# Attention and mixture of experts on one core: five pieces of zeros leave the loop, the table of slots goes through PSUM, one weight pass changes engine

## The chip, the core and the metric

The kernel runs on one NeuronCore of a Trainium2 chip. The core has TensorE (PE), which multiplies matrices into PSUM; VectorE (DVE), ScalarE (ACT) and GpSimd (POOL), which work element by element; and SyncE (SP), which here only issues DMAs. PEld is the load of PE's weights. Each engine takes its instructions in their written order and waits at semaphores; a q behind a name (SPq, POOLq) is the engine's sequencer. The metric is device time in microseconds (us), the median of the timed runs.

## The reference

Two stages. The first is attention with decay, one state per head of 64 x 64:

```
state = gamma * state + k[t] v[t]^T          # gamma per head, for each t of 768
y[t]  = scale * q[t] state                   # 4 batches, 8 heads, head size 64
```

The heads are put side by side to x, 3072 rows of 512. The second stage sends every row to two of eight experts:

```
logits = x @ w_gate;  noisy = logits + log1p(exp(x @ w_noise)) * noise
top2   = the two largest of noisy;  g = softmax over these two
out[row] = sum over the two of  g * ( relu(x[row] @ w1[e]) @ w2[e] )     # 512 -> 1024 -> 512
```

## The kernel before

**The loop.** Attention runs in 24 iterations (`for j in range(NCH)`), one for 128 time steps; six of them make a batch. An iteration issues, in this order: `qk(j+1)`, the product of k and scaled q for the next chunk (PE, L365); `q_scale(j+2)` (qs, POOL, L346) and `v_scale(j+1)` (vp, POOL, L340); the loads of chunk j+4 (SP, L278); `masked(j+1)` (am, DVE, L372); `x_store(j-3)` (SP, L428); `y_in(j)` (PE, L378); `x_total(j-1)` and `x_hi(j-1)`, the scale and the upper half of x (ACT, L412); then what the table `between` holds for this iteration; `y_mm(j)`, which adds the state's part and updates the state (PE L386 and L396, ACT L391 and L402); `x_rows(j-2)`, the transposes of x (PE L422, ACT L424) and `logits(j-2)` (PE L435 and L438); `slip()`, which issues a waiting `x_lo` (DVE, L416); then the tables `todo` and `late`. The lists are filled before the loop, so the order on every engine is written out by hand.

**What rides along.** Routing of a finished batch is cut into steps `route_a` to `route_f` and laid into later iterations, by the number `n` of the batch's last one. `table(b)` multiplies one-hot tables on PE into `LST` in PSUM (L584); `route_f(b)` adds that to `acc`, the table of slots (56 columns, SBUF); `rows_of` turns columns of it into `idx`, the row numbers that the gathers use (L599 to L602). The first weights are scaled and split as well: `w_hi` (ACT), then for each quarter of w1 `w_scaled` on POOL (L228), in place, and `w_rest` on POOL (L232).

**Zeros.** The outputs are added to by scattering DMAs, so they must hold zeros first. `zero_out(i)` writes one of twelve pieces of 512 KB from a tile of zeros, on SP's queue (L307). Eight are issued in iterations 7 and 11 to 17, four in the stage behind the loop.

**Behind the loop** the first expert's blocks follow as `units` (`early(n)` issues n of them): `mm1` on columns 0 to 384 (eight units), `mm2` for three blocks, `mm1` on columns 384 to 576 (eight), `mm2` again. Between these the last batch is routed, the other blocks are gathered (xg, POOL) and transposed by DMA into xe (SP, L709), and the next weights are loaded. Then come the seven other experts, `mm1s` and `mm2`.

**Tiles of PSUM.** `pL` is one bank that holds the logits (`PL`), the positions, `LST`, and the sums `SUM` and `XSS`; `pR` is another, in which DVE keeps small tables; its rows on the trace carry these names. On SP each DMA waits for the DMA that was issued eight before it (its lane, DMAHW0 to 7).

Of the kernel before, what the change touches and what calls it, by code (L numbers as in the profile page):

```python
# [10 lines left out]
F32 = mybir.dt.float32  # L11
# [5 lines left out]
OP = mybir.AluOpType  # L17
# [21 lines left out]
NBLK, CAP = 7, 832  # L39
CAPS = [832, 832, 832, 832, 800, 800, 768, 768]  # L40
NCOL = NBLK * E
# [54 lines left out]
def moe_kernel(ctx, tc, qT, kT, kt, vt, noise, wgn, w1, w2, ctab, qtab, xbuf, gbuf, out):  # L96
    nc = tc.nc
# [5 lines left out]
    work = ctx.enter_context(tc.tile_pool(name="work", bufs=2))  # L103
# [15 lines left out]
    def K(n):  # L119
        return ct[:, _C[n][0]:_C[n][1]]  # L120
# [10 lines left out]
    acc = consts.tile([128, NCOL], F32, name="acc")  # L131
# [12 lines left out]
    pR = psum.tile([128, 512], F32, name="pR")  # L144
# [3 lines left out]
    LST = pL[:, 280:280 + NCOL]  # L148
# [9 lines left out]
    wide = pR[:, 144:144 + NC * NL].rearrange("p (c e) -> p c e", c=NC)  # L158
    small = pR[:, 208:208 + 48]
    second_best = pR[:, 256:256 + NC]  # L160

    def pow2(ss, target, up, down=None):

# [263 lines left out]
    def x_store(j):  # L427
        nc.sync.dma_start(xbuf[128 + j * C:128 + (j + 1) * C, :], XR.pop(j))  # L428
# [158 lines left out]
    def route_f(b):  # L587
        if b == 0:
            nc.vector.tensor_copy(acc, LST)
        else:  # L590
            nc.vector.tensor_tensor(acc, acc, LST, op=OP.add)

    tk = consts.tile([128, NCOL], F32, name="tk")

    def rows_of(tk, n0, n1):

        padv = work.tile([128, NCOL], F32, name="padv")
        neg = work.tile([128, NCOL], F32, name="neg")
        nc.vector.tensor_scalar(padv[:, n0:n1], tk[:, n0:n1], 0.0, K("pad"), op0=OP.is_equal, op1=OP.mult)  # L599
        nc.vector.tensor_scalar(neg[:, n0:n1], tk[:, n0:n1], 0.0, float(TOK), op0=OP.is_lt, op1=OP.mult)  # L600
        nc.vector.tensor_tensor(neg[:, n0:n1], neg[:, n0:n1], padv[:, n0:n1], op=OP.add)
        nc.vector.scalar_tensor_tensor(idx[:, n0:n1], tk[:, n0:n1], 127.0, neg[:, n0:n1], op0=OP.add, op1=OP.add)  # L602

    def ranks():

        nc.vector.tensor_copy(cum, cump)
        m = E - 2
        n, s3, s4 = R["cum"][:, 2:E], [128, m, m], [128, m, NBLK, m]
        key = hp.tile([128, m], F32, name="key")
        nc.vector.scalar_tensor_tensor(key, n, 8.0, K("tie")[:, :m], op0=OP.mult, op1=OP.add)  # L610
        cm = hp.tile(s3, F32, name="cm")
        nc.vector.tensor_tensor(cm, key[:, None, :].to_broadcast(s3), key[:, :, None].to_broadcast(s3), op=OP.is_gt)
        rk = hp.tile([128, m], F32, name="rk")
        nc.vector.tensor_reduce(rk, cm, axis=AX.X, op=OP.add)
        pm = R["pm"] = hp.tile(s3, F32, name="pm")
        nc.vector.tensor_tensor(pm, rk[:, None, :].to_broadcast(s3),
                                K("i64")[:, :m, None].to_broadcast(s3), op=OP.is_equal)
        nc.vector.tensor_tensor(cm, pm, K("lidx")[:, None, 2:E].to_broadcast(s3), op=OP.mult)
        nc.vector.tensor_reduce(rk, cm, axis=AX.X, op=OP.add)
        nc.vector.tensor_copy(eid[:, :m], rk)  # L620
        tp = hp.tile(s4, F32, name="tp")
        v = acc[:, 2 * NBLK:].rearrange("p (e t) -> p t e", e=m)
        nc.vector.tensor_tensor(tp, v[:, None].to_broadcast(s4), pm[:, :, None, :].to_broadcast(s4), op=OP.mult)
        nc.vector.tensor_reduce(tk[:, 2 * NBLK:].rearrange("p (r t) -> p r t", r=m), tp, axis=AX.X, op=OP.add)
        rows_of(tk, 2 * NBLK, NCOL)
        nc.vector.tensor_tensor(cm, pm, K("rcap")[:, 1:, None].to_broadcast(s3), op=OP.mult)
        nc.vector.memset(capd, float(CAP))
        nc.vector.tensor_reduce(capd[:, 2:E], cm.rearrange("p r e -> p e r"), axis=AX.X, op=OP.add)
# [40 lines left out]
    def at(j, f, *a):  # L669
        todo.setdefault(j, []).append((f, a))  # L670
# [42 lines left out]
    for b in range(B - 1):  # L713
        n = (b + 1) * NC - 1
        late.setdefault(n + 2, []).append((route_a, (b,)))
        late.setdefault(n + 4, []).append((route_n, (b,)))
        steps = [(3, route_b, b), (4, route_b2, b), (4, route_c, b), (5, route_d, b),
                 (6, route_e, b, 0), (7, route_e, b, 1), (8, route_w, b)]
        if b == B - 2:
            steps = steps[:-2]  # L720
        else:
            at(n + 8, table, b)
            late.setdefault(n + 8, []).append((route_f, (b,)))
        if b == B0 - 1:

            late[n + 8].append((rows_of, (acc, 0, 3)))
            for t in range(3):
                ahead_of.setdefault(n + 9, []).append((gather, 0, t, 0, 128, B0 * S))
                at(n + 10, x_t, 0, t)
        ahead_of.setdefault(n + 5, []).append((places, b))  # L730
        for s in steps:
            between.setdefault(n + s[0], []).append(s[1:])
# [5 lines left out]
    for i in range(4):  # L738
        at(3 + i, w_load, 0, "1", i)
        at(5 + i, w_sum, 0, "1", i)  # L740
        at(10 + i, w_hi, 0, "1", i)
        between.setdefault((11, 13, 16, 18)[i], []).append((w_scaled, nc.gpsimd, 0, "1", i))
        between.setdefault((12, 14, 17, 19)[i], []).append((w_rest, 0, "1", i))
        at(8 + i, w_load, 0, "2", i)
        at(14 + i, w_sum, 0, "2", i)
        at(19 + i, w_hi, 0, "2", i)
    at(23, w_scaled, nc.scalar, 0, "2", 0)
    at(22, w_load, 1, "1", 0, 2)
    at(22, w_load, 1, "1", 2, 2)
    for i in range(8):  # L750
        at((7, 11, 12, 13, 14, 15, 16, 17)[i], zero_out, i)
    for i in range(2):
        at(10, zero_out, 12 + i)
    for j, a in ((4, (lanes16, K("lanes"))), (4, (blks16, K("blks"))), (5, (lanes.bitcast(F32), lanes16.bitcast(F32))),
# [13 lines left out]
    for j in range(NCH):  # L768
        if j == 0:
            y_in(0)  # L770
        if j + 1 < NCH:
            qk(j + 1)
        if j + 2 < NCH:
            q_scale(j + 2)
        if j + 1 < NCH:
            v_scale(j + 1)
        if j + AHEAD < NCH:
            load(j + AHEAD, "qk")
        if j + 1 < NCH:
            masked(j + 1)  # L780
        if j + AHEAD < NCH:
            load(j + AHEAD, ("v", "kt"))
        if j >= 3:
            x_store(j - 3)
        if j:
            y_in(j)
            for f, *a in ahead_of.get(j, []):
                f(*a)
            x_total(j - 1)
            x_hi(j - 1)  # L790
            slips.append(j - 1)
        for f, *a in between.get(j, []):
            f(*a)
        if j < NC - 3:
            q_table(j + 3)
        y_mm(j)
        if j >= 2:
            x_rows(j - 2)
            logits(j - 2)
        slip()  # L800
        for f, a in todo.get(j, []):
            f(*a)
        for f, a in late.get(j, []):
            f(*a)
# [251 lines left out]
    x_rows(NCH - 1)  # L1056
    logits(NCH - 1)
    x_store(NCH - 1)
    table(b - 1)
    route_f(b - 1)  # L1060
    rows_of(acc, 3, mid + 1)
    for t in range(3, mid + 1):
        gather(0, t, 0, min(128, SECOND - t * 128), (B - 1) * S)
    for t in range(3, mid + 1):
# [32 lines left out]
    early(1)  # L1097
    table(b)
    route_f(b)
    rows_of(acc, mid, 2 * NBLK)  # L1100
    for t in range(mid, NBLK):
        gather(0, t, SECOND - t * 128 if t == mid else 0)
    for t in range(mid, NBLK):
# [248 lines left out]
```

## Time and profile before

| | |
|---|---|
| three timed runs | 637.21, 634.17, 636.15 us; median 636.15 |
| profiled execution | 632.04 us, of which the trace's span is 630.3 |
| busy of the span | PE 97%, PEld 61%, DVE 72%, ACT 62%, POOL 63% |
| bytes moved | 112.90 MB, mean 179 GB/s |
| TensorE clock | 0.996 of full speed on average |
| the loop | from 0 to about 115 us |

A busy PE is not PE at its peak: its matmuls are pipelined and their ends are modelled. What a stage is worth is read from the waits in it and from how long equal pieces of work take, not from the share. A wait is put down to the last semaphore by the trace, which may hide a DMA behind an engine's name.

### The profile page before, as it was taken

How to read it: one execution, taken by the hardware profiler on the slowest of the kernel's cores; microseconds unless marked ns; L12 is line 12 of the kernel's file. 1: busy time of each engine (PE TensorE's matmuls, PEld its weight loads, DVE VectorE, ACT ScalarE, POOL GpSimd, SP SyncE). 2: the span in 40 equal slices, each digit the busy share in tenths (PEclk: the TensorE clock that was granted, in tenths of full speed). 3: DMA queues.
4: the chain of work that ended last, by engine and by line, in shares of the span. 5: the costliest groups of instructions: out<-in, count | busy, mean ns of one | idle time of the engine just before them, and what ended most of it. 6: DMA issues, size and time to landing. Idle time of an engine off the chain costs nothing.

```text
span 630.3 us, 13242 instructions
## 1 busy us (share of the span) xinstructions
PE 611.6 (97%) x5133; PEld 384.9 (61%) x5133; DVE 451.2 (72%) x952; ACT 391.8 (62%) x655; POOL 395.2 (63%) x278
## 2 busy tenths in 40 slices
PE   8999988999999999999999999999999999999995
PEld 5899877756755545554565446544654565445784
DVE  5679888788697795579657964796579557957720
ACT  4788877944456856586558655865586558556311
POOL 2657889525776885863687558657845674574154
PEclk9999999999999999999999999999999999999998
DMA  9999999867972597479546974787499549642043
GB/s 332 350 404 405 355 384 317 244 222 208 195 193 36 85 258 226 55 133 243 161 49 118 197 229 56 169 201 176 46 146 216 160 54 162 192 52 35 9 52 44
DMA packets 104321, 112.90 MB, mean 179 GB/s; under 512 B 64512, under 2 KB 78080, under 8 KB 100672
## 3 DMA queue, kind: packets, MB, share of 16 engines
q1 hardware_dynamic: 83296, 84.70, 45.5%
q0 software_dynamic: 20528, 26.90, 27.3%
q8 instruction: 41, 0.67, 0.4%
q10 hardware_dynamic: 432, 0.43, 0.2%
q14 instruction: 24, 0.20, 0.1%
HBM read 72.16 MB, written 26.47 MB: 156 GB/s over the span
## 4 chain that ended last, share of the span: by engine, by line
PE 83%; DVE 8%; DMA 3%; ACT 2%; issue 1%; POOL 1%; SPq 1%; POOLq 0%; ACTq 0%; DVEq 0%
PE pO L1001 11%; PE pO L1002 11%; PE pO L1003 11%; PE pH L900 11%; PE pH L902 10%; PE pH L901 10%; PE pA L365 2%; DVE am L372 2%; PE pY L378 2%; PE pO L992 2%; PE pT L1016 2%; PE pO L990 1%; PE pO L991 1%; PE pH L824 1%; DMA in_q<-qT 1%; PE pH L826 1%
## 5 line engine op out<-in xcount | busy, mean ns | idle before, releaser
L977 POOL DMA_INDIRECT out<-ot,idx x108 | 196.1, 1816 | 139.3 <-ACT ot L971 47.8
L1002 PE MATMUL pO<-w2l,h 128*128 128x512 f16 x336 | 127.3, 379 | 0.0
L1003 PE MATMUL pO<-w2h,h 128*128 128x512 f16 x336 | 127.3, 379 | 0.0
L1001 PE MATMUL pO<-w2h,h 128*128 128x512 f16 x336 | 127.3, 379 | 0.0
L924 DVE TENSOR_TENSOR s<-pH,s 128x416 f32<-128x416 f32 (+2 forms) x84 | 47.3, 571 | 45.0 <-PE pH L902 36.7
L697 POOL DMA_INDIRECT gx<-gbuf,idx x54 | 60.9, 1128 | 28.1 <-issue 14.5
L687 POOL DMA_INDIRECT xg<-xbuf,idx x55 | 59.2, 1076 | 20.6 <-issue 15.1
L971 ACT ACTIVATE ot<-pO,gse 128x512 f32<-128x512 f32 (+2 forms) x48 | 32.7, 683 | 59.5 <-PE pO L1003 55.9
L191 ACT ACTIVATE junk<-wst 128x1024 bf16<-128x1024 f32 x64 | 67.8, 1060 | 2.9 <-DMA wst<-w 2.8
L920 ACT ACTIVATE s<-pH 128x416 f32<-128x416 f32 (+2 forms) x84 | 40.2, 508 | 30.7 <-PE pH L902 30.6
L916 ACT ACTIVATE h<-s 128x832 f16<-128x832 f32 (+2 forms) x42 | 35.9, 871 | 35.1 <-DVE s L924 35.1
L1003 PEld LDWEIGHTS <-h 128*128 128x128 f16 x336 | 32.9, 98 | 39.7
L1001 PEld LDWEIGHTS <-h 128*128 128x128 f16 x336 | 33.0, 98 | 38.8
L1002 PEld LDWEIGHTS <-h 128*128 128x128 f16 x336 | 32.9, 98 | 38.8
L902 PE MATMUL pH<-xt,wsl 128*128 128x416 f16 (+2 forms) x168 | 56.0, 333 | 0.0
L901 PE MATMUL pH<-xt,wsh 128*128 128x416 f16 (+2 forms) x168 | 56.0, 333 | 0.0
L900 PE MATMUL pH<-xt,wsh 128*128 128x416 f16 (+2 forms) x168 | 56.0, 333 | 0.0
L220 DVE SCALAR_TENSOR_TENSOR w2l<-wst,wsc,w2h 128x1024 f16<-128x1024 f32 x28 | 35.9, 1281 | 14.1 <-ACT w2h L215 14.1
L346 POOL TENSOR_TENSOR qs<-in_q,gq 128x512 f32<-128x512 f32 x21 | 26.7, 1273 | 26.3 <-DMA in_q<-qT 17.2
L917 DVE SCALAR_TENSOR_TENSOR h<-s,h 128x832 f16<-128x832 f32 (+2 forms) x42 | 41.0, 990 | 2.7 <-ACT h L916 2.7
L858 ACT ACTIVATE xt<-s 128x832 f16<-128x832 f32 (+2 forms) x28 | 24.4, 874 | 25.1 <-DVE s L857 24.9
L900 PE MATMUL pH<-xe,w1h 128*128 128x416 f16 (+2 forms) x112 | 37.3, 333 | 0.1
(217 smaller groups left out, 1477.7 us busy)
## 6 DMA issues: line engine op xcount, KB each, us to landing
wst<-w SPq DMA_DIRECT2D x28, 1024.0 KB, 7.9
in_q<-qT SPq DMA_DIRECT2D x24, 256.0 KB, 5.7
in_k<-kT SPq DMA_DIRECT2D x24, 256.0 KB, 6.4
in_v<-vt SPq DMA_DIRECT2D x24, 256.0 KB, 5.7
xbuf<-xr SPq DMA_DIRECT2D x24, 256.0 KB, 5.6
out<-zero SPq DMA_DIRECT2D x12, 512.0 KB
in_kt<-kt SPq DMA_DIRECT2D x20, 256.0 KB, 4.5
wst<-w SPq DMA_DIRECT2D x8, 512.0 KB, 6.4
```

Of the source, the lines that this page charges most:

```text
L191: nc.scalar.activation(junk, st[:, i * 1024:(i + 1) * 1024], AF.Square, accum_out=ss[:, i:i + 1])
L687: nc.gpsimd.indirect_dma_start(out=x[:p1], out_offset=None, in_=xbuf[:128 + rows], in_offset=bass.IndirectOffsetOnAxis(ap=idx[:p1, i:i + 1 ...
L697: nc.gpsimd.indirect_dma_start(out=GX[e][:, t, :], out_offset=None, in_=gbuf[:128 + rows], in_offset=bass.IndirectOffsetOnAxis(ap=idx[:, i ...
L900: nc.tensor.matmul(p, wh, bh[:, k, :], start=start and k == 0, stop=False, skip_group_check=True)
L901: nc.tensor.matmul(p, wh, bl[:, k, :], start=False, stop=False, skip_group_check=True)
L902: nc.tensor.matmul(p, wl, bh[:, k, :], start=False, stop=(k == 1), skip_group_check=True)
L917: wait.append(lambda: nc.vector.scalar_tensor_tensor(lo, src, 0.0, hi, op0=OP.max, op1=OP.subtract))
L924: nc.vector.tensor_tensor(s[:, u], p, s[:, u], op=OP.add)
L977: nc.gpsimd.indirect_dma_start(out=out[s], out_offset=bass.IndirectOffsetOnAxis(ap=idx[:n, i:i + 1], axis=0), in_=ot[:n, s * HD:(s + 1) * ...
L1001: nc.tensor.matmul(p, a, WT["2h"][:, f, :], start=(f == 0), stop=False)
L1002: nc.tensor.matmul(p, a, WT["2l"][:, f, :], start=False, stop=False)
L1003: nc.tensor.matmul(p, c, WT["2h"][:, f, :], start=False, stop=(f == FT - 1))
```

## The change

Of the eight pieces of zeros in the loop three stay (iterations 7, 13 and 16), and five are issued behind the loop, right after the last `x_store`. `route_f` writes the sum of `acc` and `LST` to `accp`, 56 columns of `pR` in PSUM, for every batch but the first; `rows_of` and `ranks` read it there, and the inner product `padv` of `rows_of` becomes `padp`, in PSUM too. After the second and third batch `accp` is copied back to `acc`. The last of the four `w_scaled` of w1 is issued on ACT, in the same iteration. Last, `logits(0)` is issued in iteration 3, ahead of `logits(1)`, where it was issued in iteration 2.

```diff
@@ PSUM views @@
+    accp = pR[:, 264:264 + NCOL]
+    padp = pR[:, 264 + NCOL:264 + 2 * NCOL]
@@ route_f @@
-            nc.vector.tensor_tensor(acc, acc, LST, op=OP.add)
+            nc.vector.tensor_tensor(accp, acc, LST, op=OP.add)
@@ rows_of @@
-        padv = work.tile([128, NCOL], F32, name="padv")
-        nc.vector.tensor_scalar(padv[:, n0:n1], tk[:, n0:n1], 0.0, K("pad"), op0=OP.is_equal, op1=OP.mult)
+        nc.vector.tensor_scalar(padp[:, n0:n1], tk[:, n0:n1], 0.0, K("pad"), op0=OP.is_equal, op1=OP.mult)
         nc.vector.tensor_scalar(neg[:, n0:n1], tk[:, n0:n1], 0.0, float(TOK), op0=OP.is_lt, op1=OP.mult)
-        nc.vector.tensor_tensor(neg[:, n0:n1], neg[:, n0:n1], padv[:, n0:n1], op=OP.add)
+        nc.vector.tensor_tensor(neg[:, n0:n1], neg[:, n0:n1], padp[:, n0:n1], op=OP.add)
@@ ranks @@
-        v = acc[:, 2 * NBLK:].rearrange("p (e t) -> p t e", e=m)
+        v = accp[:, 2 * NBLK:].rearrange("p (e t) -> p t e", e=m)
@@ tables of the loop @@
-            late[n + 8].append((rows_of, (acc, 0, 3)))
+            late[n + 8].append((rows_of, (accp, 0, 3)))
+            between.setdefault(n + 9, []).append((nc.vector.tensor_copy, acc, accp))
-        between.setdefault((11, 13, 16, 18)[i], []).append((w_scaled, nc.gpsimd, 0, "1", i))
+        between.setdefault((11, 13, 16, 18)[i], []).append((w_scaled, nc.scalar if i == 3 else nc.gpsimd, 0, "1", i))
-    for i in range(8):
-        at((7, 11, 12, 13, 14, 15, 16, 17)[i], zero_out, i)
+    for i in range(3):
+        at((7, 13, 16)[i], zero_out, i)
@@ the loop @@
-            logits(j - 2)
+            for i in (() if j == 2 else (0, 1) if j == 3 else (j - 2,)):
+                logits(i)
@@ behind the loop @@
     x_store(NCH - 1)
+    for i in range(3, 8):
+        zero_out(i)
     table(b - 1)
     route_f(b - 1)
-    rows_of(acc, 3, mid + 1)
+    rows_of(accp, 3, mid + 1)
+    nc.vector.tensor_copy(acc, accp)
...
-    rows_of(acc, mid, 2 * NBLK)
+    rows_of(accp, mid, 2 * NBLK)
```

On DVE, iteration 19 and the start of iteration 20, where the second batch's table becomes row numbers (names ahead of the arrow are written, those behind it read). Before:

```order
L591 TENSOR_TENSOR acc<-acc,pL 128x56 [waits PE_49]
L599 TENSOR_SCALAR padv<-acc,ct 128x3 [waits DVE_49]
L600 TENSOR_SCALAR neg<-acc 128x3
L601 TENSOR_TENSOR neg<-neg,padv 128x3 [waits DVE_49]
L602 SCALAR_TENSOR_TENSOR idx<-acc,neg 128x3 [waits DVE_49]
L454 TENSOR_SCALAR pR<-upx 128x6
L457 COPY lg<-pL 128x96
L458 TENSOR_TENSOR lg<-lg,pL 128x96 [waits DVE_49]
```

And now:

```order
L593 TENSOR_TENSOR pR<-acc,pL 128x56 [waits PE_49]
L600 TENSOR_SCALAR pR<-pR,ct 128x3 [waits DVE_49]
L601 TENSOR_SCALAR neg<-pR 128x3 [waits DVE_49]
L602 TENSOR_TENSOR neg<-neg,pR 128x3 [waits DVE_49]
L603 SCALAR_TENSOR_TENSOR idx<-pR,neg 128x3 [waits DVE_49]
L456 TENSOR_SCALAR pR<-upx 128x6 [waits DVE_49]
L459 COPY lg<-pL 128x96
L460 TENSOR_TENSOR lg<-lg,pL 128x96 [waits DVE_49]
```

The steps keep their places; no step of `rows_of` has both its source table and its target in SBUF any more, and two steps have a wait for DVE itself that they had not. The copy back stands some steps later, ahead of the next batch's noise product.

On POOL, iterations 17 to 20, from the third `w_rest` of w1 to the first gather. Before:

```order
L232 TENSOR_TENSOR w1l<-wst_496,w1h 128x2x512 [waits Pool_49]
L346 TENSOR_TENSOR qs<-in_q,gq 128x512 [waits DMAHW2_49,PE_49]
L340 TENSOR_TENSOR vp<-in_v,ct 128x512 [waits DMAHW6_49]
L228 TENSOR_SCALAR wst_496<-wst_496,wsc_498 128x1024 [waits Activation_49]
L346 TENSOR_TENSOR qs<-in_q,gq 128x512 [waits DMAHW0_49,PE_49]
L340 TENSOR_TENSOR vp<-in_v,ct 128x512 [waits DMAHW4_49]
L232 TENSOR_TENSOR w1l<-wst_496,w1h 128x2x512 [waits Pool_49]
L346 TENSOR_TENSOR qs<-in_q,gq 128x512 [waits DMAHW6_49,PE_49]
L340 TENSOR_TENSOR vp<-in_v,ct 128x512 [waits DMAHW2_49]
L687 DMA xg<-xbuf,idx 128x1024 [waits DMAHW3_49,DMAHW7_49,DMAHW1_49,DVE_49]
```

And now:

```order
L234 TENSOR_TENSOR w1l<-wst_496,w1h 128x2x512 [waits Pool_49]
L348 TENSOR_TENSOR qs<-in_q,gq 128x512 [waits DMAHW6_49,PE_49]
L342 TENSOR_TENSOR vp<-in_v,ct 128x512 [waits DMAHW3_49]
L348 TENSOR_TENSOR qs<-in_q,gq 128x512 [waits DMAHW4_49,PE_49]
L342 TENSOR_TENSOR vp<-in_v,ct 128x512 [waits DMAHW0_49]
L234 TENSOR_TENSOR w1l<-wst_496,w1h 128x2x512 [waits Activation_49]
L348 TENSOR_TENSOR qs<-in_q,gq 128x512 [waits DMAHW1_49,PE_49,Pool_49]
L342 TENSOR_TENSOR vp<-in_v,ct 128x512 [waits DMAHW6_49,Pool_49]
L688 DMA xg<-xbuf,idx 128x1024 [waits DMAHW7_49,DMAHW5_49,DVE_49]
```

The pass over wst is gone from POOL, and the last `w_rest` waits for ACT where it waited for POOL.

On SP, behind the loop, from the last stored rows (`xbuf<-xr`) to the loads of the next expert's w2. Before:

```order
L428 DMA xbuf<-xr 128x1024 [waits DMAHW3_49,Activation_49]
L709 DMA_TRANSPOSE xe<-xg 128x8x128 [waits DMAHW4_49,DMASW6_49]
L709 DMA_TRANSPOSE xe<-xg 128x8x64 [waits DMAHW5_49,DMASW7_49]
L187 DMA wst_2523<-w 128x2048 [waits DMAHW6_49,Pool_49]
L187 DMA wst_2523<-w 128x2048 [waits DMAHW7_49]
```

And now:

```order
L430 DMA xbuf<-xr 128x1024 [waits DMAHW6_49,Activation_49]
L309 DMA out<-zero 256x1x512 [waits DMAHW7_49]
L309 DMA out<-zero 256x1x512 [waits DMAHW0_49]
L309 DMA out<-zero 256x1x512 [waits DMAHW1_49]
L309 DMA out<-zero 256x1x512 [waits DMAHW2_49]
L309 DMA out<-zero 256x1x512 [waits DMAHW3_49]
L710 DMA_TRANSPOSE xe<-xg 128x8x128 [waits DMAHW4_49,DMASW6_49]
L710 DMA_TRANSPOSE xe<-xg 128x8x64 [waits DMAHW5_49,DMASW7_49]
L189 DMA wst_2523<-w 128x2048 [waits DMAHW6_49,Pool_49]
L189 DMA wst_2523<-w 128x2048 [waits DMAHW7_49]
```

The five pieces stand between the last stored rows and the transposes of blocks 3 and 4.

## Rows read from the trace of the kernel before

**Rows 1.** The page's 40 slices of the span: busy tenths of TensorE, of the DMA engines.

```profile
PE   8999988999999999999999999999999999999995
DMA  9999999867972597479546974787499549642043
```

**Rows 2.** Windows: from:to, length, busy us (instructions) of five engines, clock, DMA share, GB/s.

```profile
33.41:58.21 24.80, 24.80 (x471) 23.22 (x470) 20.21 (x84) 22.45 (x47) 13.18 (x13) 1.00 1.04 405
58.21:85.37 27.16, 25.16 (x481) 23.30 (x480) 23.02 (x95) 22.73 (x45) 22.73 (x15) 1.00 1.06 370
85.37:114.25 28.88, 24.54 (x467) 22.51 (x466) 26.63 (x107) 22.31 (x45) 25.96 (x21) 1.00 1.04 326
160.00:620.00 460.00, 459.88 (x2903) 260.88 (x2902) 325.25 (x490) 277.50 (x424) 294.63 (x199) 1.00 0.67 133
```

**Rows 3.** Timeline of TensorE, the table: start, duration, instruction, count, [idle before, releaser].

```profile
95.88 0.47 PE L584 MATMUL pL<-bb,a 128*128 128x56 f16 x12
```

**Rows 4.** Chain of waits, 73 to 84 us: start, duration, what.

```profile
73.74 7.12 DMA in_q<-qT
...
82.32 1.16 PE pA L365 x16
```

**Rows 5.** Waits of TensorE, 58 to 116 us: total us, times, longest.

```profile
PE pA L365 <- POOL qs L346: 3.9, 6, 1.2
PE pL L407 <- DVE lg L458: 1.9, 1, 1.9
PE pH L824 <- DMA xe<-xg: 0.7, 1, 0.7
PE pY L378 <- DVE x L416: 0.4, 1, 0.4
```

**Rows 6.** Timeline of GpSimd, iterations 18 and 19.

```profile
92.62 2.85 POOL L228 TENSOR_SCALAR wst<-wst,wsc 128x1024 f32<-128x1024 f32 x1
95.43 1.28 POOL L346 TENSOR_TENSOR qs<-in_q,gq 128x512 f32<-128x512 f32 x1
...
97.66 2.14 POOL L232 TENSOR_TENSOR w1l<-wst,w1h 128x1024 f16<-128x1024 f32 x1
```

**Rows 7.** Timeline of VectorE, `rows_of` twice, and a step from PSUM to PSUM.

```profile
97.22 2.60 DVE L599 TENSOR_SCALAR padv<-acc,ct 128x3 f32<-128x3 f32 x1
99.74 0.15 DVE L600 TENSOR_SCALAR neg<-acc 128x3 f32<-128x3 f32 x1
...
112.04 0.16 DVE L550 TENSOR_SCALAR pR<-pR 128x1 f32<-128x1 f32 x1
...
125.42 1.12 DVE L599 TENSOR_SCALAR padv<-acc,ct 128x2 f32<-128x2 f32 x1
```

**Rows 8.** Timeline of ScalarE: copy of iteration 18, and a `w_scaled` of w2.

```profile
92.80 1.02 ACT L424 ACTIVATE xr<-pX 128x1024 f16<-128x1024 f16 x1 [0.73 <-DMA xbuf<-xr]
...
116.78 1.16 ACT L226 ACTIVATE wst<-wst,wsc 128x1024 f32<-128x1024 f32 x1
```

**Rows 9.** Chain of waits, from the first gather to the first `mm1`.

```profile
102.59 4.90 DMA xg<-xbuf,idx
...
110.85 4.75 DMA xe<-xg
115.74 0.32 PE pH L824
```

**Rows 10.** Timeline of TensorE, iterations 2 and 3.

```profile
20.58 0.19 PE L435 MATMUL pL<-wg,x 128*128 128x32 f16 x1 [0.57 <-DVE p2m L167]
...
20.87 1.16 PE L365 MATMUL pA<-qs,in_k 64*128 64x128 f32 x16
...
22.36 1.09 PE L378 MATMUL pY<-am,vp 128*64 128x128 f32 x16 [0.33 <-DVE x L416]
```

**Rows 11.** Timeline of SyncE and TensorE: transposes of blocks 3 and 4, their first use.

```profile
130.59 2.55 SPq L709 DMA_TRANSPOSE xe<-xg  x2
...
150.76 0.25 PE L824 MATMUL pH<-xe,w1h 128*128 128x192 f16 x1
```

## The prediction

> **What bounds the kernel now.** I read the 40 slices first [rows 1]. TensorE (PE) stands at 8 or 9 everywhere, so busy shares say little by themselves; the DMA row is at 9 over the first seven slices, which is the attention loop of 24 iterations, and moves about below that afterwards. Then I cut the loop into equal pieces: the windows of [rows 2] begin with the transposes of iterations 5, 11, 17 and 23, so each of the first three holds six iterations, one batch each. They last 24.80, 27.16 and 28.88 us. In the first PE is busy to the last hundredth, and its 24.80 us are what six iterations need; the last row shows 459.88 of 460 us busy between 160 and 620. So PE sets the pace up to 58 us and again behind the loop, and between the two it waits. A microsecond that the loop loses there is a microsecond of the end, and one that is won is won at the end, as long as the stage behind it keeps its place.
>
> What the second and third batch need of PE: the first one's 24.80, and 0.47 for one table product that the first has not [rows 3], 25.3; the third has one qk product less (1.16 [rows 4]), 24.1. They lose 27.16 - 25.3 = 1.9 and 28.88 - 24.1 = 4.8 us. Who is waited for stands in [rows 5]: POOL's qs six times (3.9 us), the lg of VectorE (DVE) once (1.9), the loop's transposed rows xe at the loop's end (0.7), x_lo (0.4): 6.9 us, which agrees with 1.9 + 4.8.
>
> Behind POOL's qs stands another cause each time. At 73.74 the chain of waits goes through the load of a q, 7.12 us to its landing, then POOL's qs, and into qk at 82.32 [rows 4]: that is the DMA queue, at a share of 1.04 to 1.06 in all three batches [rows 2]. Later it is POOL itself: w_scaled of 2.85 us, then qs at once behind it at 95.43 [rows 6], POOL being busy 25.96 of 28.88 us. And lg was late because DVE stood in padv for 2.60 us [rows 7].
>
> **The change part by part.** *Five pieces of zeros leave the loop.* Each is 0.52 MB, at the 405 GB/s of the first batch 1.3 us of the DMA engines. By the iterations that issued them four lie in the second batch and one in the third. The second moved 370 GB/s x 27.16 us = 10.0 MB; without four pieces 7.9 MB, or 19.6 us at 405 GB/s, and this is below the 25.3 us of PE. The third: 326 x 28.88 = 9.4 MB, less 0.5, 22 us. So the loads no longer bind in either. What is late next in the second batch: DVE and POOL have 23.0 and 22.7 us of work in it [rows 2], both under PE's need, so PE is next, with the one x_lo wait of 0.4 us left. I take 25.3 + 0.4 = 25.7 us, a gain of 1.4; ends: 0 (the waits only change their owner) and 1.9.
>
> *w_scaled of piece 3 goes from POOL to ScalarE (ACT).* POOL loses 2.85 us in iteration 18 [rows 6], and qs of iteration 19 can start as soon as its q has landed. On ACT the same form took 1.16 us [rows 8]. ACT is busy 22.31 of 28.88 us in that batch, and it waited 0.73 us for a store just after, in iteration 18 [rows 8], so it has room; but the copies queued behind it (the square sum, U, xr) come 1.1 us later. U is used by the next iteration's y_mm, which stands behind its qk and y_in; I cost this at nothing, and at up to 1.1 us if that cover is gone.
>
> *The table through PSUM.* padv is DVE's tensor_scalar on three columns, SBUF to SBUF, and took 2.60 us at 97.22 and 1.12 us at 125.42, where the next one of the same form, neg, took 0.15 [rows 7]. It began while POOL worked without a pause and ended at 99.82, when POOL's w1l ended (97.66 + 2.14 = 99.80) [rows 6]; it is a wait for POOL, not work. With source and target in PSUM, the nearest row is 0.16 us for a tensor_scalar from pR to pR [rows 7]. So 2.44 us go in iteration 19. Added are one copy of 56 columns (0.16, by the same row) and two more waits of DVE for itself, about 0.1 each, an estimate from neg, which has no such wait and began 0.08 before padv's end (99.74 against 99.82). Net -2.1 us of DVE. Bounds: if PSUM helped nothing, 0 and +0.4; if all waiting goes, -2.4. The second place, 1.12 us, is hidden: its gather has 14 us in hand (below), so nothing there.
>
> [...]
>
> The third batch then. DVE is its fullest engine: 26.63 of 28.88 us, 24.5 after the change, more than the 24.1 of PE. It also stood 2.25 us idle for partners (ACT's x_hi, PE's qk); most of that is order of work and stays, I take 1.8. So 24.5 + 1.8 = 26.3, rounded to 26.4: a gain of 2.5, ends 0.5 (only a part of the padv stall, the rest taken by the later w_scaled) and 4.8 (PE's need).
>
> *End of the loop.* The first gather goes out at 102.59 behind POOL's work of iteration 20, lands after 4.90 us, three transposes follow, and mm1 starts at 115.74 [rows 9], of which PE idled 0.7 [rows 5]. Its index comes 2.4 us earlier and POOL is 2.85 us lighter, so this chain shortens its start by more than the loop shortens its end: I take 0.6 of the 0.7; ends 0 and 0.7.
>
> *The logits of row block 0 move from iteration 2 to 3.* In iteration 2 they waited 0.57 us for DVE and took 0.29 (20.58 to 20.87); but y_in at 22.36 waited for x_lo, not for them [rows 10]. So they cost nothing there, and in iteration 3, where PE is the bound, they cost 0.29. I take +0.3; ends 0 and 0.3.
>
> *The five pieces behind the last stored rows.* 2.6 MB, 6.5 us. They are issued on SP's queue at about 126, ahead of the transposes of blocks 3 and 4 (issued 130.59 to 133.14). The DMA row stands at 6 in that slice [rows 1]. mm1 reads these blocks first at 150.76 [rows 11]. With the 4.75 us that a transpose took under load [rows 9] they were there by 138, and with 6.5 us more by 144.4: 6 us are left. Cost 0; if the cover is gone, every microsecond beyond it counts.
>
> Sum: -1.4 - 2.5 - 0.6 + 0.3 = -4.2 us. Against the profiled execution's own 632.04 us (span 630.3 and 1.74 around it) that is 627.8. The three timed runs lie at 634.17 to 637.21, so the profiled one is 4.1 below their median; from the median, 636.15 - 4.2 = 632.0 us.
>
> **The rivals.** *A, the waits only change their owner.* Where PE waited for a late q it would wait for DVE's work instead, which stands in the same iterations. Then only DVE's own 2.1 us come, less the 0.3 of the logits: -1.8, 634.4 us. For it: 26.63 of 28.88 us busy [rows 2]. Against it: the second batch, where DVE has 4.1 us free.
>
> *B, PE's need is reached in both batches* (-1.9 - 4.8 - 0.7 + 0.3 = -7.1, 629.0). For it: the first batch shows 24.80 of 24.80 us with DMA just as full. Against it: DVE's 24.5 us of work and its dependences in the third batch.
>
> *C, slower: the zeros starve the second half of expert 0.* The transposes of blocks 3 and 4 stand behind 6.5 us of zeros in their own queue, and share the engines with the gathers that feed them. If each of five pieces took the 7.12 us of the loop's worst load, one after the other, the blocks would land at 138 + 35.6 = 173.6, 22.8 us after mm1's need; with 4.2 us won that is +18.6, 655 us. It is slower than before from 10 us of delay beyond the cover. For it: the zeros are issued ahead of those transposes on one queue. Against it: that queue waits only for the DMA eight places back, so eight are under way at a time, as in the loop, where 7.12 us was the time of one among them.
>
> *D, nothing changes*, because the loads were not what delayed the q's and POOL's saved 2.85 us fall into waiting: only the padv term less the rest, within 1 us of 636.15. For it: POOL's qs also needs the slot that y_mm frees.
>
> **How the numbers follow.** Chances: forecast 0.62, A 0.20, B 0.10, D 0.05, C 0.03. The forecast's own range, from half of the three gains to all but a microsecond of PE's need, is 630.3 to 633.9. For 8 in 10 it is widened to B below and to A and most of D above, with the runs' own scatter of 1.5 us to each side: 629.0 to 636.0. What can be told from no change here is 0.5%, 3.2 us, so faster means below 633.0. Of the forecast's 0.62 some 0.44 lie there, all of B, and 0.04 of A: 0.58. Slower (above 639.3) is C and a little scatter, 0.04. The rest, 0.38, is the same.
>
> **What would show it.** In the profile after: padv's line at 0.2 us or less in both places; the second and third batch at 25.7 and 26.4 us; in_q landing in under 6 us after iteration 12; no wait of PE for POOL's qs over 0.3 us; mm1's first product at about 111.5 without waiting for xe; and the DMA row full around 122 to 128 with mm1 of columns 384 to 576 not waiting. The prediction is wrong if the third batch stays at 28, or if mm1 waits for xe later on.

## The result, and the profile after

The changed kernel takes 629.18 us (median of six runs, 628.55 to 632.24), the kernel before 636.89 (six runs, 634.17 to 638.64) beside it: ratio 0.9889, 95% interval 0.9860 to 0.9918. Medians here are over all timed runs, while a ratio leaves out the slow ones, those more than 1.5% above the fastest of their kernel (five of the twelve of e4 below, whose medians alone would give 0.993). The changed kernel is faster, inside the range and 2.8 us below the forecast. That is the outcome; the way there is less tidy. The profiled execution of after took 629.79 us (span 627.9), that of before 632.04 (630.3): the two traces differ by 2.3 us, the medians by 7.7. The traces can explain only the 2.3, and each trace is one execution.

The windows of the changed kernel begin at the same transposes as [rows 2]. Columns: from:to, length, then busy us (instructions) of PE, PEld, DVE, ACT and POOL, PE's granted clock, DMA share, GB/s.

```profile
34.17:58.98 24.81, 24.81 (x472) 23.23 (x470) 20.22 (x84) 22.46 (x47) 12.47 (x12) 1.00 1.05 402
58.98:84.34 25.36, 24.94 (x481) 23.30 (x480) 23.45 (x98) 23.26 (x47) 23.55 (x16) 1.00 1.06 364
84.34:110.30 25.96, 24.40 (x467) 22.51 (x466) 23.96 (x105) 22.88 (x44) 22.25 (x19) 1.00 1.02 293
```

The second batch went from 27.16 to 25.36 us and the third from 28.88 to 25.96; the first, which PE alone fills, did not move. TensorE's waits of that stretch (line, engine and tile waited for: us in total, times, longest) against [rows 5]:

```profile
PE pA L367 <- POOL qs L348: 1.0, 2, 0.7
PE pY L380 <- DVE x L418: 0.4, 1, 0.4
PE pY L380 <- DVE i L483: 0.3, 1, 0.3
PE pL L409 <- ACT w2h L217: 0.3, 1, 0.3
```

6.9 us have become 2.0: qs 3.9 to 1.0, and lg and xe are gone. VectorE's first `rows_of` (start, duration, instruction), which stands against [rows 7]:

```profile
95.33 0.23 DVE L600 TENSOR_SCALAR pR<-pR,ct 128x3 f32<-128x3 f32 x1
95.59 0.16 DVE L601 TENSOR_SCALAR neg<-pR 128x3 f32<-128x3 f32 x1
```

2.60 us have become 0.23. `mm1` starts at 110.96 where it started at 115.74: 4.8 us won. At the end of the span 2.4 of them are left; 2.1 are lost between the tails of the first two experts. The chain of waits of the changed kernel behind the loop (start, duration, what):

```profile
134.51 8.76 DMA gbuf<-gateb
...
144.02 1.24 POOL gx L698
145.57 3.60 DMA xg<-xbuf,idx
149.19 1.23 SPq L710
150.51 8.20 DMA xe<-xg
...
159.49 7.25 DMA xg<-xbuf,idx
...
190.24 0.34 PE pH L903
```

The store of the gates (30 KB) takes 8.76 us to land, and the gather of the gates on POOL waits for it. Behind it on POOL stand the gathers of the last blocks of expert 0 and, in one row with them, those of expert 1. The chain ends at 190.24, where TensorE waits 1.63 us for a sum of expert 1's rows; a chain names what came last, not what the time would be without it, and e4 below tries that. Before, the same two gathers on POOL (with the idle time ahead of each) read:

```profile
143.74 0.97 POOL L697 DMA_INDIRECT gx<-gbuf,idx  x1 [12.10 <-DMA out<-zero]
147.01 1.74 POOL L687 DMA_INDIRECT xg<-xbuf,idx  x1 [2.30 <-DMA out<-zero]
```

There the store went out at 139.29, later than now, and the gather could follow 4.4 us later. So the gathers stand at almost the same absolute time in both kernels (147.01 and 145.57), although `mm1` starts 4.8 us earlier. What stood ahead of that store in the changed kernel is on SyncE's queue:

```profile
121.63 5.87 SPq L309 DMA_DIRECT2D out<-zero  x5
127.59 4.91 SPq L710 DMA_TRANSPOSE xe<-xg  x2
132.60 1.01 SPq L189 DMA_DIRECT2D wst<-w  x2
134.51 0.38 SPq L536 DMA_DIRECT2D gbuf<-gateb  x1
```

These are the five pieces of zeros, and two loads of weights that the pieces hold up: they go out 1.9 us ahead of the store, where in the kernel before it was 6.1 us (133.23 and 139.29). From 128 to 135 us the DMA share is 1.01 in the changed kernel and 0.54 in the kernel before.

### The profile page after: what moved, and what is told of

Same layout as the page of the kernel before. It is cut to its first block, busy times and chain, and to the rows that moved or that the text cites. A ratio compares the mean times of both kernels' runs of the same rounds, so it can differ in the third digit from the quotient of the medians.

```text
span 627.9 us, 13243 instructions
## 1 busy us (share of the span) xinstructions
PE 612.9 (98%) x5133; PEld 385.1 (61%) x5133; DVE 448.2 (71%) x954; ACT 392.3 (62%) x656; POOL 390.3 (62%) x277
## 4 chain that ended last, share of the span: by engine, by line
PE 79%; DVE 9%; DMA 7%; ACT 2%; issue 2%; POOL 1%; SPq 1%; POOLq 0%; DVEq 0%; ACTq 0%
PE pH L903 11%; PE pH L905 10%; PE pH L904 10%; PE pO L1006 10%; PE pO L1005 10%; PE pO L1004 10%; PE pY L380 2%; PE pA L367 2%; DMA xe<-xg 2%; PE pY L388 2%; DVE am L374 2%; DMA xg<-xbuf,idx 2%; PE pO L995 2%; PE pO L994 2%; PE pO L993 2%
## 5 line engine op out<-in xcount | busy, mean ns | idle before, releaser
L1004 PE MATMUL pO<-w2h,h 128*128 128x512 f16 x336 | 127.3, 379 | 0.0
L688 POOL DMA_INDIRECT xg<-xbuf,idx x55 | 56.9, 1035 | 20.6 <-issue 15.3
L919 ACT ACTIVATE h<-s 128x832 f16<-128x832 f32 (+2 forms) x42 | 35.9, 871 | 35.1 <-DVE s L927 35.1
L903 PE MATMUL pH<-xt,wsh 128*128 128x416 f16 (+2 forms) x168 | 56.0, 333 | 1.8 <-ACT s L923 1.8
L1004 PEld LDWEIGHTS <-h 128*128 128x128 f16 x336 | 32.9, 98 | 38.8
L222 DVE SCALAR_TENSOR_TENSOR w2l<-wst,wsc,w2h 128x1024 f16<-128x1024 f32 x28 | 35.9, 1280 | 14.1 <-ACT w2h L217 14.1
L903 PE MATMUL pH<-xe,w1h 128*128 128x416 f16 (+2 forms) x112 | 37.3, 333 | 0.1
```

The lines of the kernel that those rows point to most:

```text
L688: nc.gpsimd.indirect_dma_start(out=x[:p1], out_offset=None, in_=xbuf[:128 + rows], in_offset=bass.IndirectOffsetOnAxis(ap=idx[:p1, i:i + 1 ...
L903: nc.tensor.matmul(p, wh, bh[:, k, :], start=start and k == 0, stop=False, skip_group_check=True)
L1004: nc.tensor.matmul(p, a, WT["2h"][:, f, :], start=(f == 0), stop=False)
```

## The experiments

They ran on three further chips, four kernels on each. There the kernel before takes 10 to 13 us more than on the first chip and the changed one 16 to 17, so each ratio is to the kernel before on the same chip, and profiles are compared within a chip where that is possible. A profile is one execution: the third batch of the kernel before lasts 28.88, 36.73 and 32.80 us in its three, so a difference of a few microseconds between two profiles shows little by itself. In the table, "rows" is the time from `mm1`'s first product to the first gather of rows for the last three blocks of expert 0, "transposes" to the first transpose of these rows, "expert 0" to the first transpose pT of its tail; all from the profiled run, in us. "Clock" is the mean granted clock of the timed runs (of the profile for the two in brackets).

| run | chip | median | ratio | batch 2 | batch 3 | mm1 | rows | transposes | expert 0 | clock |
|---|---|---|---|---|---|---|---|---|---|---|
| before | first | 636.89 | 1 | 27.16 | 28.88 | 115.74 | 31.3 | 35.5 | 69.4 | (0.996) |
| after | first | 629.18 | 0.9889 | 25.36 | 25.96 | 110.96 | 34.6 | 38.2 | 69.7 | 0.997 |
| e1, before | 2nd | 647.87 | 0.9989 [0.9951, 1.0028] | 27.31 | 36.73 | 124.23 | 31.3 | 35.9 | 72.4 | 0.991 |
| e2, zeros back in the loop | 2nd | 649.17 | 1.0000 [0.9958, 1.0043] | 30.47 | 32.36 | 121.77 | 31.4 | 35.7 | 73.9 | 0.994 |
| e3, zeros moved only | 2nd | 647.63 | 0.9961 [0.9925, 0.9997] | 25.41 | 34.60 | 118.07 | 33.3 | 37.4 | 77.2 | 0.990 |
| e4, five pieces left out | 2nd | 644.76 | 0.9899 [0.9854, 0.9944] | 25.36 | 30.66 | 115.59 | 31.4 | 35.7 | 70.3 | 0.995 |
| e11, after | 3rd | 646.09 | 1.0003 [0.9972, 1.0034] | 25.85 | 30.64 | 116.01 | 34.6 | 37.9 | 75.6 | 0.993 |
| e8, gates behind rows | 3rd | 642.02 | 0.9920 [0.9887, 0.9953] | 25.82 | 29.74 | 114.27 | 31.4 | 38.1 | 71.8 | 0.997 |
| e10, table in SBUF | 3rd | 644.41 | 0.9966 [0.9936, 0.9997] | 25.37 | 30.35 | 115.51 | 34.5 | 37.8 | 76.0 | 0.994 |
| e9, pass on POOL | 3rd | 647.38 | 1.0001 [0.9968, 1.0035] | 25.50 | 30.86 | 115.61 | 34.0 | 38.7 | 74.6 | 0.993 |
| e14, after | 4th | 645.09 | 0.9963 [0.9934, 0.9992] | 25.84 | 29.87 | 115.36 | 34.6 | 38.4 | 73.6 | 0.995 |
| e15, before, one run | 4th | 644.19 | | 30.21 | 32.80 | 121.91 | 31.3 | 35.5 | 69.4 | (0.993) |
| e12, zeros behind store | 4th | 644.60 | 0.9971 [0.9941, 1.0002] | 25.49 | 31.83 | 116.62 | 31.4 | 39.1 | 73.6 | 0.996 |
| e13, three moved | 4th | 640.85 | 0.9905 [0.9872, 0.9938] | 27.13 | 29.55 | 115.38 | 31.4 | 39.1 | 71.6 | 0.998 |

**e1 and e15, the kernel before once more** (no edit).

> The kernel before, unchanged, for a second profile: its profiled execution (632.04 us) was shorter than all its timed runs. Theory 1 (the loop waits for loads, and how long differs from execution to execution): the second and third batch of the loop again last over 27 and 28 us, and together with the first they may differ by one to four us from the first profile. Rival (the loop is bound by the engines' own order of work): all three batches within 0.3 us of 24.8, 27.2 and 28.9.

> The kernel before, for its profile on this chip beside the other three. Theory: first three batches about 24.8, 27 and 29 us or more, TensorE's wait for lg 1.9 us or more, gather of expert 1's first rows 31.3 us after mm1's first product. Rival (the loop of the kernel before loses nothing to lg here): third batch equal to that of the changed kernel.

On these chips the kernel before loses more in its loop than [rows 2] showed, mostly in the same two places (e1 also stands three times for 0.6 us, which its trace puts down to nothing). In e15 TensorE waited 4.0 us for qs and 3.9 for lg, and its windows show what follows such a wait:

```profile
80.00:84.00 4.00, 1.84 (x44) 1.69 (x40) 1.92 (x9) 3.85 (x9) 1.40 (x2) 0.96 1.05 393
84.00:86.00 2.00, 2.00 (x18) 1.78 (x20) 0.85 (x5) 0.88 (x1) 2.00 (x2) 0.50 1.00 362
...
100.00:104.00 4.00, 0.56 (x12) 0.31 (x6) 3.93 (x6) 0.93 (x1) 3.63 (x3) 1.00 1.07 398
104.00:108.00 4.00, 3.58 (x49) 3.47 (x49) 3.86 (x23) 1.73 (x5) 3.24 (x4) 0.57 0.78 184
```

The granted clock (third figure from the right) falls to 0.50 after TensorE has stood: behind a wait of 2.15 us for qs at 83.92 and one of 3.86 us for lg at 104.42. The 16 products behind the first took 2.08 us where they take 1.16. So these waits were paid for again after they had ended. In e3 the clock is 0.61 from 100 to 104 us, behind an lg wait of 4.13 us, and the 16 products of L386 there take 1.68 us (1.07 in e15 ahead of its lg wait). In e14, with waits for qs of up to 1.2 us, it stays at 1.00. In the trace of before on the first chip the lg wait was 1.9 us, and every window of [rows 2] is at 1.00.

**e2 and e3, the zeros alone.** e2 is the changed kernel with the eight pieces back where they were; e3 is the kernel before with the same lines the other way round, and nothing else of the change.

```diff
-    for i in range(3):
-        at((7, 13, 16)[i], zero_out, i)
+    for i in range(8):
+        at((7, 11, 12, 13, 14, 15, 16, 17)[i], zero_out, i)
...
-    for i in range(3, 8):
-        zero_out(i)
```

> The changed kernel with the eight pieces of zeros back in iterations 7 and 11 to 17 and none behind the last stored rows; table in PSUM, pass on ScalarE and logits stay changed. Theory 1 (the loads are the first cause): second batch again near 27 us, in_q landing up to 7 us, the third batch near 26.5 to 27.5 because padv and the pass are gone from it; time 2 to 3 us under the kernel before, so 4 to 5 us over the changed one. Rival (POOL and DVE are the cause, the zeros are not): second batch under 26, time as the changed kernel's.

> The kernel before with the zeros alone moved as in the change. Theory 1: second batch near 25.5 us, third near 28 (padv still 2.6, the pass still on POOL); behind the loop the next expert's rows come late as in the changed kernel; time 2 to 4 us under the kernel before. Rival (zeros are not the cause): no difference beyond 1 us.

The second batch belongs to the zeros: 25.41 us in e3 and 30.47 in e2. TensorE's waits for qs in that batch of e2, and the window of e2's third batch (columns as above):

```profile
PE pA L367 <- POOL qs L348: 5.3, 4, 2.0
...
88.51:120.87 32.36, 27.14 (x468) 24.30 (x466) 25.57 (x111) 24.03 (x47) 23.19 (x20) 0.96 0.99 310
```

The third batch needs the other parts as well. With the zeros alone moved (e3) it lasts 34.60 us, with a wait for lg of 4.1 us and the clock of 0.61 behind it; with the zeros alone put back (e2) 32.36, without that wait, but with 2.6 us of stops that the trace puts down to nothing and a mean clock of 0.96; with the five pieces left out and all else changed (e4, the same chip) 30.66. The time of e2 equals that of the kernel before, where 2 to 3 us less were expected; e3 is some 2.5 us below it, at the edge of what its interval can tell. VectorE and POOL in e3 (rows of both engines in order of time, with the instructions between left out):

```profile
94.10 1.05 POOL L340 TENSOR_TENSOR vp<-in_v,ct 128x512 f32<-128x512 f32 x1
94.66 4.81 DVE L599 TENSOR_SCALAR padv<-acc,ct 128x3 f32<-128x3 f32 x1
95.10 2.13 POOL L232 TENSOR_TENSOR w1l<-wst,w1h 128x1024 f16<-128x1024 f32 x1
...
97.18 1.27 POOL L346 TENSOR_TENSOR qs<-in_q,gq 128x512 f32<-128x512 f32 x1
...
98.40 1.05 POOL L340 TENSOR_TENSOR vp<-in_v,ct 128x512 f32<-128x512 f32 x1
```

padv begins while POOL works and ends at 99.47, when POOL's fourth instruction in a row ends at 99.45. It stands longer than the 2.60 us of [rows 7], but the earlier loads are not shown to be the reason: in e1, with the zeros in the loop, the four steps of `rows_of` stand for 0.52, 2.17, 1.18 and 0.97 us, as long together, and TensorE waits 3.7 us for lg. Neither half alone is worth much here: ratios 0.9961 and 1.0000.

**e10 and e9, the other two parts undone.**

```diff
@@ e10, against after @@
-            nc.vector.tensor_tensor(accp, acc, LST, op=OP.add)
+            nc.vector.tensor_tensor(acc, acc, LST, op=OP.add)
...
-        nc.vector.tensor_scalar(padp[:, n0:n1], tk[:, n0:n1], 0.0, K("pad"), op0=OP.is_equal, op1=OP.mult)
+        nc.vector.tensor_scalar(padv[:, n0:n1], tk[:, n0:n1], 0.0, K("pad"), op0=OP.is_equal, op1=OP.mult)
@@ e9, against after @@
-        between.setdefault((11, 13, 16, 18)[i], []).append((w_scaled, nc.scalar if i == 3 else nc.gpsimd, 0, "1", i))
+        between.setdefault((11, 13, 16, 18)[i], []).append((w_scaled, nc.gpsimd, 0, "1", i))
```

> The changed kernel with the table of slots back in SBUF (padv and acc as before); zeros, weight pass and logits stay as changed. Theory (the wait of VectorE in padv is a bound of its own beside the loads): padv and neg together at 2 us or more again in the third batch, TensorE waits 2 to 4 us for lg, third batch 28 us or more, 2 to 2.5 us slower than the changed kernel, ratio 0.993. Rival (with one weight pass gone from GpSimd there is nothing left for padv to wait for): padv under 0.5 us, time equal to the changed kernel's.

> The changed kernel with the weight pass of piece 3 back on GpSimd. Theory (the pass is a bound only for the qs behind it, and VectorE no longer waits for GpSimd): one wait of TensorE for qs of 1 to 2.5 us comes back in iteration 19, third batch 1 to 2 us longer, ratio 0.991 to 0.993. Rival (GpSimd has slack once loads land earlier, so the pass costs nothing on either engine): time equal to the changed kernel's within 0.5 us.

In e10 the stall came back as expected, in two instructions:

```profile
95.44 0.95 DVE L601 TENSOR_SCALAR padv<-acc,ct 128x3 f32<-128x3 f32 x1
96.31 1.08 DVE L602 TENSOR_SCALAR neg<-acc 128x3 f32<-128x3 f32 x1
```

TensorE waited 1.7 us for lg, but the third batch (30.35 us) and the time did not get worse than in e11 (30.64 us): the expected 2 us of time did not come. On that chip the changed kernel loses the same time to other short waits there (qs 1.9, den 0.8, 1.1 us put down to nothing). With the table in PSUM the lg wait is 0.3 us or nothing in every profile, also in e9, where the pass is back on POOL; with the table in SBUF it is 1.7 with the pass on ScalarE and 1.9 to 4.1 with it on POOL. e9 equals e11 in time: its rival was right, the pass by itself is worth nothing that can be measured. So the table takes the lg wait away, and that this shortens the third batch is not shown by undoing it alone. Only with table and pass both undone (e3 against e4) is that batch longer, by 3.9 us, in one profile of each.

**e4, the cost of the five pieces.**

```diff
-    for i in range(3, 8):
-        zero_out(i)
```

> The changed kernel without the five pieces behind the last stored rows: these rows of the outputs are not zeroed, nothing else is left out. In the changed kernel 2 us that the loop had won were lost at expert 1, where TensorE waited 1.6 us for a copy. Theory 1 (the five pieces hold up SP's transposes, the next loads and the gate store, POOL stands behind the gate gather, and so expert 1's rows come late): POOL's first gate gather behind the loop no later than 140, expert 1 without that wait, 2 us under the changed kernel. Rival (expert 1's rows are bound by the gathers and transposes themselves, whatever the zeros do): the wait stays, time within 0.5 us of the changed kernel.

Without them the gather of the gates goes out 28.2 us after `mm1`'s start (28.0 before, 33.1 after), the rows are gathered at 31.4 and first transposed at 35.7, as in the kernel before, and expert 0 takes 70.3 us. So the five pieces do hold the gates, these rows and their transposes up, by 2 to 5 us. But the other half of the expectation failed. TensorE in e4, from `mm1` to the tail of expert 1:

```profile
PE pH L903 <- ACT s L923: 1.1, 1, 1.1
```

The wait at expert 1 stays, though it is shorter than the 1.8 us of after, and expert 1 takes 66.0 us (66.2 after, 64.0 before). The last transpose of its rows goes out 60.0 us after `mm1`'s start, as late as in after (60.2; 56.4 before). In e10, with the pieces in place, expert 1 takes 64.0 us and does not wait at all. The time does not settle it: the ratio of e4 is below those of the changed kernel on two other chips (1.0003 and 0.9963), but the changed kernel did not run on this one, and in the profiles e1 and e4 take the same 136.4 us from `mm1` to the tail of expert 1. So the delay is shown, and what it costs is not.

**e11 and e14, the changed kernel once more** (no edit).

> The changed kernel once more, as the yardstick for the three beside it. Theory (loads and VectorE's wait for GpSimd both bound the loop, and a part of the gain is given back behind it): ratio 0.989, batches about 24.8, 25.4 and 26 us or, if this chip's extra idle time in the third batch comes again, up to 30; no wait of TensorE for lg over 0.5 us. Rival (the 1.1 % were this one chip's): ratio 0.995 or more.

> The changed kernel as yardstick on this chip. Theory (the loop gains about 4 us on every chip, and what the stretch behind it gives back differs by how long TensorE then stands): gather of expert 1's first rows 34.6 us after mm1's first product, ratio between 0.989 and 1.0. Rival (the first chip's 0.989 is the rule): ratio 0.986 to 0.992.

Ratios 1.0003 and 0.9963, not 0.9889. On the fourth chip both kernels have a profile. The loop wins more there, 121.91 to 115.36 us at `mm1`, and no window of e14 from 60 to 260 us is below full clock. But expert 0 takes 4.2 us longer than in e15 and expert 1 another 1.9, and of the gain 0.5 us is left at expert 1's tail (255.57 and 255.11). What TensorE does in that stretch can be bad; in e11:

```profile
156.00:160.00 4.00, 1.77 (x14) 1.02 (x13) 0.64 (x2) 0.33 (x1) 2.45 (x3) 0.90 1.00 209
160.00:164.00 4.00, 2.61 (x17) 2.46 (x17) 3.02 (x5) 1.11 (x4) 1.89 (x2) 0.50 1.00 215
164.00:168.00 4.00, 4.00 (x21) 2.32 (x20) 2.60 (x9) 1.48 (x2) 3.30 (x3) 0.75 1.18 199
```

TensorE, VectorE and ScalarE all stand while POOL gathers rows and SyncE issues transposes, and the clock falls afterwards. TensorE waits for `h`, not for rows; the trace names no cause for the stop of all three, and it is not settled here. Stops of all three, of 0.4 to 1.9 us, stand in the 80 us behind `mm1`'s start in e1 to e3, e10 to e12 and e14, in the kernel before as in changed ones; in e4, e8, e9, e13 and e15 there is none.

**e8, e12 and e13: where the gates and the zeros stand.** e13 holds both edits, and `logits(j - 2)` of row block 0 in iteration 2 as before. `route_w` issues the store of the gates.

```diff
@@ e8, against after @@
-    gates(0, 3, (B - 1) * S)
     route_e(b, 0)
...
     for t in range(mid, NBLK):
         gather(0, t, SECOND - t * 128 if t == mid else 0)
+    gates(0, 3, (B - 1) * S)
@@ e12, against after @@
     x_store(NCH - 1)
-    for i in range(3, 8):
-        zero_out(i)
...
     route_w(b - 1)
-    for i in range(8, 12):
+    for i in range(3, 12):
         zero_out(i)
```

> The gather of the gates, which waits for their store, now stands behind the gathers of the next expert's rows on GpSimd. Theory (the store of the gates lands late behind five pieces of zeros, the gather of the gates waits for it at the head of GpSimd's queue, and so the next expert's rows come no earlier than before): the first of those gathers goes out some 1.5 us or more earlier than in the changed kernel, TensorE's waits at L903 for ScalarE's s shrink from 1.8 us to under 0.5, and the time falls by 1.5 to 2 us, ratio to the kernel before 0.986. Rival (the rows were bounded by their own data or by the DMA engines, not by the gates): the gathers start earlier but their transposes land at the same time, L903 waits as long, time equal to the changed kernel's within 0.5 us.

> The changed kernel, but the five pieces of zeros stand behind the store of the gates, with the four pieces that were there already, not ahead of the transposes of blocks 3 and 4. Theory (the zeros ahead of that store made it land late; the gather of the gates waited for it and the rows of expert 1 stood behind that gather): measured from mm1's first product, the gather of the gates goes out at about 28 us instead of 33, the first gather of expert 1's rows at about 31.4 instead of 34.6, and the time falls by 1.5 to 3 us below the changed kernel on the same chip, ratio to the kernel before 0.992 if the changed kernel gives 0.997 here. Rival (nine pieces in a row merely move the delay to the rows' own transfers, in the same stretch of the DMA queues): gathers earlier, transposes of expert 1 landing no earlier, time equal to the changed kernel's within 0.5 us.

> As the run before, and besides the gather of the gates behind the gathers of expert 1's first rows, and the logits of row block 0 back in iteration 2. Theory: the two moves of the stretch behind the loop pay for the same wait, so the second adds at most 0.5 us; the logits were costed at 0.3 us; together 2 to 4 us below the changed kernel, ratio to the kernel before about 0.991. Rival (the gather of the gates is a delay of its own, whatever the store does): 1.5 us or more below the run before.

e8 is 4 us below e11, with intervals that do not touch; e12 equals e14; e13 is 4 us below both, though its interval overlaps e14's by a hair. So the place of the zeros alone is worth nothing and the place of the gate gather is worth some 4 us: the rival of e13 was right (its third edit, the logits, was not run by itself). (The gathers called expert 1's rows in these expectations begin with three for the last blocks of expert 0; the seven of expert 1 follow, in e8 and e13 behind the gate gather.) POOL and SyncE in e12 show what the zeros' place does:

```profile
140.61 10.61 SPq L309 DMA_DIRECT2D out<-zero  x9
...
144.79 0.97 POOL L698 DMA_INDIRECT gx<-gbuf,idx  x1 [12.89 <-DMA out<-zero]
148.02 1.74 POOL L688 DMA_INDIRECT xg<-xbuf,idx  x1 [2.26 <-DMA out<-zero]
...
155.68 4.34 SPq L710 DMA_TRANSPOSE xe<-xg  x3
```

The gate gather now goes out 28.2 us after `mm1`'s start and the first rows 31.4, as expected, but their transposes stand behind nine pieces on SyncE's queue and go out at 39.1, later than e14's 38.4. But the time does not hang on these transposes: in e8 too the rows leave at 31.4 and are transposed at 38.1, in e13 at 39.1, and both are 4 us faster. The rival of e8 foresaw the late transposes, and that TensorE's waits for the sum at L903 stay (two before 200 us, 1.8 us in all), but not the time. In the profiles e8 and e13 differ in expert 0: 71.8 and 71.6 us against 75.6 and 73.6. In e13 no window of 4 us from 60 to 260 us is below full clock, but that is also so in e14, and the mean clock of e8's profile is 0.997, as that of e14's. Over all timed runs their mean clock is 0.997 and 0.998, against 0.993 and 0.995 of the changed kernel. At e11's span a hundredth of clock is 6.4 us of TensorE's time, so these 0.003 are an estimated 2 of the 4 us. Where the rest lies, and why the order of the gathers does this, is not shown. e13's profiled run was its slowest, 644.27 us, and e12's its fastest, 639.83, so their windows cannot be set against each other. Both versions are faster than the kernel before and the changed one where they ran; on the first chip they were not run.

## Why the prediction was right, point by point

- **Second batch, -1.4**: measured -1.8, and e2 and e3 show that taking the five pieces out causes it. **Third batch, -2.5**: -2.9 on the first chip. padv fell by 2.37 us, 2.44 were taken. That lg would not be late again held in every profile with the table in PSUM; that the 2.9 us come from it is argued, since e10 without it was no slower. One sign named ahead did not come: TensorE still waits for qs, twice, up to 0.7 us where 0.3 were allowed. The step neg reads PSUM in 0.16 us and read SBUF in 0.15.
- **End of the loop, -0.6**: -0.8; `mm1` waits no more for xe.
- **Logits, +0.3**: the loop is 0.8 us later by iteration 5; 0.6 of it is there in iteration 2 already, the rest fits the term. It was not tried by itself.
- **ACT pass, 0**: held (e9). POOL's saved 2.85 us, which were expected to free a qs, are not seen in the time either.
- **Five pieces, 0**: this is the step that came out wrong. The prediction asked for one reader of the delayed transposes, `mm1` on columns 384 to 576, and that cover held (it waits 0.4 us, for `h`). It did not follow SyncE's queue and the DMA engines further: the small store of the gates, POOL's gather that waits for it, and the ten gathers of rows behind that one. Measured: rows 3.3 us later against `mm1`, and e4 shows that the pieces do this. On the first chip 2.1 us are lost between the tails of the two experts (64.0 us before, 66.2 now). The trace of after leads back from there to the gates, but without the pieces (e4) expert 1 took 66.0 us, so how much of the 2.1 is theirs stays open. Rival C had the place nearly right and the size far off; it named the blocks, not the gates.
- **The rivals**: 629.18 us is the time of B (629.0) rather than the forecast's, but B's mechanism came only in part: the second batch reached TensorE's need (25.36 against 25.3), the third stayed 1.9 us above it (25.96 against 24.1).
- **The base**: the sum of -4.2 was set on the median of before, 4.1 us above its profile. The profile alone gives -2.3, less than forecast by those 2 us; the medians give -7.7. The missing 5.4 us lie in executions of before that have no profile on the first chip. On the second and fourth chip the kernel before is seen to lose such time: the mean clock of its profile is 0.987 in e1 and 0.993 in e15, against 0.996 on the first chip, and e15's windows show it behind the waits; on all three further chips its timed runs have a mean clock of 0.990 to 0.991. That the first chip's timed runs did the same is argued, not shown. So the time came out right partly because two errors, a cost left out and a gain not counted, stand against each other. On the third and fourth chip the change is worth 0 to 0.4%.
- **Slips in the sums**, none of which moves the range: 26.3 was put down as 26.4; the 6.9 us of waits hold 0.7 for xe that lie behind the windows, so 6.2 stand against 6.7; the forecast's own range comes to 630.1 to 634.2 by its terms; and in C the 10 us are the delay with the cover in it, 4.2 beyond it.

## What to carry to other kernels

When DMAs are put ahead of others on a queue, follow the queue to the last thing that waits behind it: small stores (the 30 KB of the gates took 8.76 us to land) and the engine whose next gather waits for them, not only the big reader that comes to mind. Then try what the delay costs: here it was real, and putting the zeros behind the store (e12) did not change the time. Try a gather that waits for a late store behind those that do not wait; here that was worth some 4 us. Where the clock fell behind a wait of TensorE, the wait cost more than its length (in e15 16 products took 2.08 us where they take 1.16), so compare the clock of the timed runs as well as one trace.

## What the runs showed of the hardware

- VectorE's wait for POOL did not always end with the POOL instruction that it met. In e3 padv stood through four in a row (4.81 us, none of them over 2.13); in e15 three instructions of `rows_of` stood one after another (POOL's rows of the same stretch below them):

```profile
99.15 2.29 DVE L599 TENSOR_SCALAR padv<-acc,ct 128x3 f32<-128x3 f32 x1
101.35 1.31 DVE L600 TENSOR_SCALAR neg<-acc 128x3 f32<-128x3 f32 x1
102.69 0.96 DVE L601 TENSOR_TENSOR neg<-neg,padv 128x3 f32<-128x3 f32 x1
...
99.28 2.13 POOL L232 TENSOR_TENSOR w1l<-wst,w1h 128x1024 f16<-128x1024 f32 x1
101.37 1.26 POOL L346 TENSOR_TENSOR qs<-in_q,gq 128x512 f32<-128x512 f32 x1
102.59 1.04 POOL L340 TENSOR_TENSOR vp<-in_v,ct 128x512 f32<-128x512 f32 x1
```

  Each ends within 0.03 us of a POOL instruction: w1l at 101.41, qs at 102.63, vp at 103.63. With the table in PSUM the wait is gone (0.23 us for the step in padv's place and 0.16 for neg in after; the same in e9, where both end while POOL's vp is under way, 95.39 to 96.43). Why SBUF and PSUM differ here is not shown.
- The same kernel takes 636.9 us on one chip and 646.9 to 649.5 on three others. From expert 1's tail to the end the profiles of before and after give 381.1 and 381.0 us on the first chip, 386.8 and 388.3 on the fourth, with waits of TensorE for ScalarE's `h` (1.4 us at L1001 in e15, 1.9 at L1004 in e14) that the first does not have. What makes the difference is open.
